# A new order table for a fused attention and gated MLP kernel: query-maxima splits on GpSimd, a weight load issued later

## The chip, the cores and the metric

The kernel runs on one core of a Trainium2 chip. The metric is the time of one execution on the device in microseconds (us); the number that counts is the median of several runs. Engine names are those of the profile: PE is TensorE (PEld its weight loads), DVE is VectorE, ACT is ScalarE, POOL is GpSimd, SP is SyncE, which here only issues transfers.

## The reference, cut to what matters

Two stages follow each other. The first is a linear attention over 8 batches, 8 heads, 576 tokens and head size 64, with a feature map of 2 x 128 features:

```python
def phi(x):
    proj = np.einsum('bhsd,df->bhsf', x, w_phi)
    proj = proj - np.max(np.abs(proj), axis=-1, keepdims=True)
    return np.concatenate([np.exp(proj), np.exp(-proj)], axis=-1)
q_p, k_p = (phi(q), phi(k))
kv = np.einsum('bhsf,bhsd->bhfd', k_p, v)
z = np.sum(k_p, axis=2)
num = np.einsum('bhsf,bhfd->bhsd', q_p, kv)
den = np.einsum('bhsf,bhf->bhs', q_p, z)[..., None] + 1e-06
```

Its output, heads side by side, is `x` of 8 x 576 x 512. The second stage is a gated MLP: `h = relu(x @ w_in)` with 1024 columns, split into `u` and `v` of 512; `v` is normalized over its columns, mixed over the tokens by the 576 x 576 matrix `w_spatial` plus a bias, multiplied with `u`, and multiplied by `w_out`.

## The kernel before

All work is written out as a list of words, `ORDER` (lines 17 to 153). The last lines of the kernel take the words one by one and call the function of that name, so the order of the words is the order of the instructions in each engine's queue; engines run their queues in order and wait for each other by semaphores that the framework sets. A word is a name, its indices, after a colon the buffers or PSUM banks that it takes, and after an @ the engine, where there is a choice: `qs.0.1.0:2@V` splits the maxima of batch 0, token half 1, head half 0 into buffer 2 on DVE. @V is DVE, @A ACT, @P POOL, @S SP. `BUFS` gives the number of buffers of each kind; a word that takes a buffer waits until the last reader of the earlier content is done.

The 576 tokens of a batch are four blocks of 128 and a tail of 64; the tails of two batches are worked on together (words that end in t, index g for the pair). The words of one batch, in the order of their data:

- Loads. `lk` and `lq` (lines 364 to 369) load keys and queries as bf16 from POOL's queue, `lv` values from SP's, `lkt`, `lqt`, `lvt` the tails. Batch 0 comes in pieces: `lkf` loads a quarter of the keys from SP, `ckf` casts it; `lq0` is half of the queries. `lin.0`, `lin.1` and `lout` load w_v, w_u and w_out, `lsp` the first 512 rows of the spatial weights, `lspt` (line 432) their last 64, all from POOL.
- Turns. `tk` and `tq` (line 491) transpose a piece on PE, `tkc` and `tqc` copy it out of PSUM. Later batches use transposes by transfer instead, `xk` and `xq` (line 481), from SP.
- Keys. `kp` (line 544) projects with w_phi into two banks, `km` (line 551) takes the absolute maxima on DVE, `ke` the two exponentials on ACT, `kem` (line 559) the exponentials of the maxima, with which `vs` (line 605) scales the values. `vsz` fills the columns for the sums, `vst` and `vstz` do the same for the tails. `kv` (line 628) multiplies features and values, `kvc` copies the result.
- Queries. `qp` projects, `qm` takes maxima, `qs` (line 650) splits the maxima into two bf16 parts: a cast and a subtraction, each of 128 x 8. `qt` turns the parts on PE, `qc` copies them, `qf` (line 660) projects again, transposed, and subtracts the maxima by matmuls, `qe` takes the exponentials. `qn` (line 712, matmuls at line 719) multiplies with kv, `qr` and `qx` divide.
- MLP. `tx`/`txc` on PE or `xx` by transfer transpose x; `vm` (line 832) computes v, `vr` its relu, `vb`, `va`, `vx`, `vw`, `vy`, `vn` normalize it; `um` and `ur` compute u; `sm` mixes over the tokens, `sg` gates, `om` multiplies by w_out, `oc` copies into one of five buffers `ob`, `od` stores it.
- `warm.n.w:b` is n filler matmuls of w columns on zeros into bank b. `zvst`, `zmhl`, `zsp`, `zvnt`, `csel`, `csel2`, `cphi`, `chalf` and `cident` make constants; `spt`/`spc` turn the spatial weights, `spb` adds their bias rows.

Around the start the queues stand like this. SP: the four quarters of the first keys, w_phi after the first, then the tails and values. POOL: the identity, `lspt`, the cast of the second key quarter (`ckf.1`), the queries of batch 0, `lsp`, `lk.1`, the last cast, `lin.0`, `lq.1`, `lin.1`, and only then products. DVE does the four splits of the main blocks of batch 0; POOL does the split of the tail and all splits of later batches.

The last output products (`om`) of the table come one after the other, each copied by ACT or DVE and stored by SP; the very last is `om.7.1`, copied by ACT.

Of the kernel before, what the change touches and what calls it, by code (L numbers as in the profile page):

```python
# [22 lines left out]
kpt.0:2,3 ket.0.0:0 cqt.0:0@V tqt.0:0 warm.2.512:1 tk.0.1.1:1 km.0.1:2 tqtc.0:0@V tkc.0.1.1@V csel2@V kem.0.2:1
kmt.0:3 ke.0.1.0:2 warm.3.512:0 warm.3.128:0 tq.0.0.0:0 ke.0.1.1 tqc.0.0.0:2@V tq.0.0.1:1 warm.11.128:1 qpt.0:6,7
kem.0.1:2 tqc.0.0.1@A warm.2.512:0 warm.1.128:0 qp.0.1.0:0,1 ke.0.2.1 zmhl.1@V tq.0.1.0:4 lvt.0:0@S lq.1:0 qmt.0:0
lv.0.1:1@S qp.0.0.0:6,7 tq.0.1.1:5 lbs:0@S lkt.1:0@S lin.1 qm.0.1.0:1 ket.0.1 tqc.0.1.0:3@A qm.0.0.0:2 kp.0.3:2,3
# [6 lines left out]
qc.0.1.1:2@V qet.0.1 qe.0.0.1.0:3 lv.1.0:3@S vs.0.3.1@P kv.0.3:4 kvc.0.3@A qe.0.0.1.1 qn.0.1.0:2,3 qr.0.0.0:0  # L33
lqt.1:1@S vsz.0.2@P qx.0.0.0:0 qf.0.1.1:6,7 vs.0.2.1@P qe.0.1.1.0:4 kv.0.2:4 qr.0.1.0:1 spt.4:0 tkc.1.0.0:4@V
qx.0.1.0:1 tk.1.0.1:1 lq.2:1 kvc.0.2@V spc.4@V lv.1.1:0@S qe.0.1.1.1 qnt.0.0:2,3 ckt.1:0@P qn.0.0.1:4,5 qrt.0.0:2
qxt.0.0:0 tk.1.1.0:0 vst.0.1.0@P lv.2.1:1@S qr.0.0.1:0 tkc.1.0.1@A qn.0.1.1:6,7 kp.1.0:2,3 qx.0.0.1 txt.0.0:1
qr.0.1.1:1 qx.0.1.1 tkc.1.1.0:5@V tx.0.0:4 tk.1.1.1:5 ke.1.0.0:4 txc.0.0:0@V warm.3.128:1 kp.1.1:6,7 tx.0.1:0
txtc.0.0:0@A km.1.0:1 tkc.1.1.1@V vst.0.1.1@V vm.0.0:1 xq.2.0:6 vmt.0.0:4 ke.1.1.0:0 txc.0.1@V spb@P tx.0.2:5 ke.1.1.1
warm.3.128:5 tx.0.3:0 km.1.1:2 vr.0.0:0@A kem.1.0:0 vm.0.1:1 tq.1.1.0:6 txc.0.3@V ke.1.0.1 txc.0.2@A vrt.0.0:1@A
tq.1.0.0:7 kem.1.1:2 tq.1.0.1:0 vm.0.2:2 vb.0.0:0 tq.1.1.1:3 va.0.0:0 lk.2:2 vr.0.1:2@A tqc.1.0.0:0@A vr.0.2:3@A  # L40
xq.2.1:1 tqc.1.0.1@A tqc.1.1.0:2@V tqc.1.1.1@A vm.0.3:1 vbt.0.0:1 vb.0.1:2 kp.1.3:4,5 vat.0.0:1 lout vs.1.0.0:1@P
qp.1.0.0:6,7 spt.3:0 vr.0.3:4@A va.0.1 vs.1.0.1@P vxt.0.0 vb.0.2:3 vs.1.1.0:0@P spc.3@A qp.1.0.1:2,3 vsz.1.1@P
vsz.1.0@P chalf@P vwt.0.0:0 ke.1.3.0:2 qm.1.0.0:1 vs.1.1.1@P lvt.1:0@S xk.2.0:3 xk.2.1:4 vx.0.0 va.0.2:2 um.0.0:1
kp.1.2:6,7 qm.1.0.1:2 vyt.0.0 kv.1.0:0 qs.1.0.0:1@P vb.0.3:0 ur.0.0:1@A ke.1.3.1 qt.1.0.0:1 lv.2.0:3@S spt.1:2 spt.0:3
qc.1.0.0:1@V spc.1@V um.0.3:1 vw.0.0:1 kvc.1.0:1@A ke.1.2.0:3 ke.1.2.1 tkt.1:0 va.0.3 ur.0.3@A vx.0.1 kv.1.1:2 vy.0.0
km.1.3:3 tktc.1:0@V vnt.0.0:0@P um.0.1:4 spt.2:5 spc.0@A spc.2@A vn.0.0:1@P kem.1.3:1 kvc.1.1@V qp.1.1.0:0,1 km.1.2:0
qm.1.1.0:3 vw.0.1:2 qf.1.0.0:2,3 qp.1.1.1:6,7 um.0.2:5 qs.1.0.1:0@P vy.0.1 kem.1.2:3 qt.1.0.1:0 qe.1.0.0.0:1 vn.0.3@P
vn.0.1@P vn.0.2@P sm.0.3:1 qm.1.1.1:0 qc.1.0.1:0@V qs.1.1.0:2@P ur.0.2@A sg.0.3 qt.1.1.0:5 sm.0.0:0 qf.1.0.1:6,7
qc.1.1.0:2@V vs.1.3.0:2@P lk.3:0 vsz.1.3@P qe.1.0.0.1 ur.0.1@A xk.3.1:5 qs.1.1.1:1@P qp.2.0.0:2,3 qe.1.0.1.0:0
vs.1.2.0:3@P qe.1.0.1.1 qp.2.1.0:4,5 vsz.1.2@P qm.2.0.0:1 qm.2.1.0:2 sg.0.0 sm.0.1:1 qt.1.1.1:2 vs.1.2.1@P sg.0.1  # L50
vs.1.3.1@P sm.0.2:3 qs.2.1.0:0@P qn.1.0.0:6,7 kv.1.2:4 qc.1.1.1:1@V lq.3:1 kv.1.3:5 kvc.1.3@A qp.2.0.1:0,1 qr.1.0.0:2
sg.0.2 kvc.1.2@A qf.1.1.0:2,3 qn.1.0.1:4,5 qx.1.0.0:2 qm.2.0.1:3 qe.1.1.0.0:3 qnt.0.1:6,7 qf.1.1.1:0,1 qe.1.1.0.1
# [10 lines left out]
qc.2.1.1:0@V qe.2.1.0.1 lv.4.1:0@S kp.2.3:4,5 vnt.0.1@P qe.2.0.0.0:0 km.2.3:1 qe.2.0.0.1 lq.5:0 vn.1.0:2@P vw.1.1:0
km.3.0:2 um.1.3:1 um.1.1:0 vsz.2.0@P od.0.1@S ur.1.3@A ur.1.1@A vy.1.1 vn.1.1@P vn.1.3@P vn.1.2@P qp.3.0.0:2,3
kem.2.3:1 ke.2.3.0:3 ke.3.0.0:2 smt.0.1:1 vs.2.0.1@P xk.4.1:6 vs.2.1.0:0@P sm.1.2:0 qm.3.0.0:2 sgt.0.1 qp.3.0.1:2,3
sg.1.2 smt.0.0:1 vs.2.1.1@P qm.3.0.1:1 ke.3.0.1 vsz.2.1@P ke.2.3.1 kem.3.0:2 vs.2.3.0:3@P sm.1.0:0 qf.2.0.1:6,7
qpt.1:2,3 vsz.2.3@P kem.2.2:3 vs.2.3.1@P vs.2.2.0:2@P xk.4.0:4 sg.1.0 sgt.0.0 kp.3.1:4,5 kv.2.0:0 lv.3.1:3@S
qe.2.0.1.0:2 od.0.2@S kvc.2.0:2@A vs.2.2.1@P qe.2.0.1.1 kv.2.1:1 kvc.2.1@A kv.2.3:0 qmt.1:3 km.3.1:0 kvc.2.3@A
qp.3.1.1:2,3 kp.3.3:6,7 vsz.2.2@P qm.3.1.1:0 ke.3.1.0:1 ke.3.1.1 sm.1.3:1 kv.2.2:0 lq.4:1 km.3.3:1 qn.2.0.0:2,3
kvc.2.2@A sg.1.3 qr.2.0.0:1 sm.1.1:4 ke.3.3.0:4 qs.3.0.0:2@P qx.2.0.0:1 kem.3.3:1 qt.3.0.0:5 qc.3.0.0:2@V kem.3.1:3  # L70
qn.2.0.1:0,1 qr.2.0.1:2 omt.0:5 vs.3.0.0:1@P qp.3.1.0:2,3 ke.3.3.1 oct.0:3@A kp.3.2:6,7 vs.3.0.1@P qx.2.0.1 od.0.0@S
sg.1.1 qm.3.1.0:2 ke.3.2.0:3 qst.1:1@P qf.2.1.1:0,1 vs.3.1.0:0@P om.1.1:4 vst.1.1.0@P om.1.2:5 qe.2.1.1.0:3 km.3.2:2
oc.1.1:0@A qe.2.1.1.1 xx.2.0:2 oc.1.2:4@V om.1.3:2 qtt.1:3 ke.3.2.1 qn.2.1.0:4,5 oc.1.3:2@V qct.1:1@V qf.3.0.0:0,1
qr.2.1.0:0 qn.2.1.1:2,3 qs.3.1.0:0@P ckt.2:0@V qx.2.1.0:2 vs.3.1.1@P qr.2.1.1:1 qx.2.1.1 om.1.0:6 qe.3.0.0.0:4
qft.1:4,5 qs.3.0.1:2@P kem.3.2:0 vs.3.3.0:3@P vsz.3.1@P kp.4.0:2,3 kv.3.1:7 oc.1.0:1@V vsz.3.0@P km.4.0:3 vsz.3.3@P
vs.3.3.1@P xq.5.1:0 qe.3.0.0.1 qet.1.0:0 kv.3.0:6 vm.2.1:0 qet.1.1 qt.3.0.1:1 kvc.3.0:0@V kvc.3.1@A odt.0@S ke.4.0.0:0
# [978 lines left out]
```

## Time and profile before

| | |
|---|---|
| median of 3 runs | 264.83 us (264.47 to 265.33) |
| the profiled execution | 264.12 us |
| its span, first to last instruction | 262.3 us |
| PE busy | 247.9 us, 94% of the span |
| DVE busy | 220.1 us, 84% |
| ACT busy | 200.7 us, 77% |
| POOL busy | 168.4 us, 64% |
| bytes moved | 41.91 MB, 160 GB/s in the mean |

Busy times are sums of instruction times. PE's are modelled at their ends and overlap, so PE may show busy while it only finishes; the fillers count as busy too. A row of the timeline has the start, the duration, the engine, the line, the operation, the output and inputs by the names of the program, the count, and in brackets the idle time of that engine before it and what ended it. The line is often that of a helper: 267 is every copy on DVE or POOL, 265 every copy on ACT, 547 every projection, 552 every maximum.

### The profile page before, as it was taken

Reading aid. Unit: us, or ns where it says so; the run is one execution under the profiler, and the core shown is the slowest. Engines: PE = TensorE matmul, PEld = TensorE weight load, DVE = VectorE, ACT = ScalarE, POOL = GpSimd, SP = SyncE. Lnnn points to the kernel's source line nnn. Section 1 sums busy time; section 2 is a strip of 40 time slices with the busy share of each in tenths; the row PEclk is TensorE's granted clock in tenths of the full one; section 3 lists DMA queues with packets and bytes.
Section 4 is the critical chain, followed back from the end, with each engine's and each line's share of the span. In section 5 each row is a group of like instructions: output and inputs, shape, how many; then the busy total and the mean of one; then the engine's idle time right before and its main releaser. Section 6 shows DMA issues by size and latency. Waiting matters only on the chain.

```text
span 262.3 us, 8256 instructions
## 1 busy us (share of the span) xinstructions
PE 247.9 (94%) x3292; PEld 151.6 (58%) x3329; DVE 220.1 (84%) x441; ACT 200.7 (77%) x332; POOL 168.4 (64%) x300
## 2 busy tenths in 40 slices
...
GB/s 162 212 203 224 225 219 262 152 161 214 122 173 199 181 236 142 130 145 175 157 219 314 153 146 171 60 182 193 189 177 81 90 75 2 40 82 0 122 189 214
DMA packets 82076, 41.91 MB, mean 160 GB/s; under 512 B 50995, under 2 KB 77299, under 8 KB 82037
## 3 DMA queue, kind: packets, MB, share of 16 engines
...
q8 instruction: 26, 0.43, 0.7%
...
## 4 chain that ended last, share of the span: by engine, by line
PE 61%; DVE 16%; DMA 14%; issue 3%; ACT 3%; SPq 1%; DVEq 0%; ACTq 0%
PE banks L834 8%; PE banks L959 8%; PE banks L945 8%; PE banks L930 8%; DMA tf<-in_q_dram 6%; PE banks L547 5%; PE banks L636 5%; DVE mk L552 4%; PE banks L719 4%; DMA T<-ld 4%; DMA out_dram<-ob 3%; DVE mq L552 3%; PE banks L663 3%; PE banks L667 2%; PE banks L947 2%
## 5 line engine op out<-in xcount | busy, mean ns | idle before, releaser
L672 ACT ACTIVATE qf<-banks 128x1024 bf16<-128x1024 f32 x72 | 70.2, 1030 | 7.5 <-PE banks L667 6.7
L556 ACT ACTIVATE kf<-banks 128x1024 bf16<-128x1024 f32 x64 | 64.1, 1034 | 7.8 <-PE banks L547 3.8
L605 POOL TENSOR_TENSOR vs<-v,em 128x512 bf16<-128x512 f32 x63 | 64.9, 1039 | 7.9 <-ACT em L562 6.3
L552 DVE TENSOR_REDUCE mq<-banks 128x8 f32<-128x1024 f32 x36 | 43.2, 1213 | 2.9 <-PE banks L547 2.6
L552 DVE TENSOR_REDUCE mk<-banks 128x8 f32<-128x1024 f32 x36 | 43.3, 1213 | 1.4 <-PE banks L547 0.8
L945 PE MATMUL banks<-w_spT,vn 128*128 128x512 bf16 x119 | 32.1, 380 | 0.5
L930 PE MATMUL banks<-xT,w_u 128*128 128x512 bf16 x128 | 32.2, 380 | 0.1
L843 POOL TENSOR_TENSOR rs<-mv,neghalf 128x2 f32<-128x2 f32 (+2 forms) x21 | 13.9, 666 | 28.5 <-DVE mv L840 28.3
L834 PE MATMUL banks<-w_v,xT 128*128 128x512 bf16 x117 | 30.9, 379 | 0.6
L959 PE MATMUL banks<-w_out,uT 128*128 128x512 bf16 x119 | 29.8, 379 | 0.5
L954 DVE TENSOR_TENSOR uT<-banks,uT 128x512 bf16<-128x512 f32 x32 | 21.3, 680 | 6.8 <-PE banks L947 6.7
L547 PE MATMUL banks<-wphi,T 64*128 64x128 bf16 x512 | 23.9, 218 | 2.6 <-ACT uT L271 1.5
L271 ACT ACTIVATE vr<-banks 128x512 bf16<-128x512 f32 (+1 forms) x27 | 16.3, 604 | 11.8 <-PE banks L834 7.8
L849 POOL TENSOR_SCALAR vn<-vr,rs,mv 128x512 bf16<-128x512 bf16 x30 | 23.0, 774 | 1.3 <-POOL mv L846 0.2
L636 PE MATMUL banks<-vs,kf 128*128 128x66 bf16 x512 | 23.3, 194 | 0.1
L636 PEld LDWEIGHTS <-kf 128*128 128x128 bf16 x512 | 21.4, 97 | 2.6
L861 DVE BATCH_NORM_STATS2 st<-vr 128x6 f32<-128x512 bf16 x32 | 21.5, 682 | 1.4 <-ACT vr L271 1.1
L547 PEld LDWEIGHTS <-T 64*128 64x128 bf16 x512 | 15.5, 94 | 12.2 <-issue 9.5
L732 DVE TENSOR_TENSOR x<-banks,rc 128x512 bf16<-128x512 f32 x32 | 21.9, 686 | 0.7
L265 ACT COPY ob<-banks 128x512 f32<-128x512 f32 x19 | 11.0, 591 | 14.7 <-PE banks L959 14.2
L638 PE MATMUL banks<-vst,kft 128*128 128x66 bf16 x128 | 20.9, 192 | 0.0
L719 PE MATMUL banks<-kv,qf 128*128 128x66 bf16 x512 | 20.7, 193 | 0.0
...
## 6 DMA issues: line engine op xcount, KB each, us to landing
v<-in_v_dram SPq DMA_DIRECT2D x16, 512.0 KB, 9.1
...
ld<-in_k_dram POOLq DMA_DIRECT2D x7, 512.0 KB, 9.3
ld<-in_q_dram POOLq DMA_DIRECT2D x7, 512.0 KB, 9.2
...
```

What stands on the lines that cost most here:

```text
L547: nc.tensor.matmul(out=bank(banks[y])[:, n * F:(n + 1) * F], lhsT=xT[halves[y], n, :], rhs=wphi[halves[y], :], start=True, stop=True)
L552: nc.vector.tensor_reduce(out=out_, in_=pp.rearrange("p y (n f) -> p y n f", f=F), axis=AX.X, op=ALU.max, apply_absolute_value=True)
L556: nc.scalar.activation(out=kf[:, s].rearrange("p y n f -> p y (n f)"), in_=pp, func=AF.Exp, bias=0.0, scale=(1.0, -1.0)[s])
L605: ENG[e].tensor_tensor(out=at["vs", (b, j)][:, s, :, 0:D], in0=at["v", (b, j // 2)][:, (j % 2) * n:(j % 2 + 1) * n, :], in1=at["em", (b, j ...
L636: nc.tensor.matmul(out=pv[:, hh, s, :], lhsT=kf[:, s, c % 2, 2 * hh + c // 2, :], rhs=w[:, s, NB * hh + c, :], start=(c == 0), stop=False)
L672: nc.scalar.activation(out=at["qf", u][:, s].rearrange("p y n t -> p y (n t)"), in_=at["pq", u], func=AF.Exp, bias=0.0, scale=(1.0, -1.0)[s])
L719: nc.tensor.matmul(out=at["pn", u][:, y, n, :], lhsT=f[:, s, y, n, :], rhs=at["kv", b][:, hg * HH + n, s, :], start=(s == 0), stop=(s == 1))
L834: nc.tensor.matmul(out=bank(place)[r], lhsT=lhs[:, kc, r], rhs=w_v[:, kc, :], start=(kc == 0), stop=(kc == KC - 1))
L849: ENG[e].tensor_scalar(out=out_, in0=in_, scalar1=rs, scalar2=mv, op0=ALU.mult, op1=ALU.add)
L930: nc.tensor.matmul(out=bank(place).rearrange("p (c t) -> p c t", c=NB), lhsT=w_u[:, kc, dc * P:(dc + 1) * P], rhs=at["xT", b][:, :, kc, :] ...
L945: nc.tensor.matmul(out=bank(place), lhsT=at["vn", b][:, c, cs], rhs=w_spT[:, c, 0:T0], start=(c == 0), stop=False)
L959: nc.tensor.matmul(out=bank(place), lhsT=at["uT", b][:, dc, c * P:(c + 1) * P], rhs=w_out[:, dc, :], start=(dc == 0), stop=(dc == KC - 1))
```

## The change

Only the table is another. It holds the same words but for the fillers, in another order, with some other buffers and banks, and with other engines for some words. By the fillers it has 1,504 words instead of 1,498: 41 filler matmuls of 512 columns instead of 39, and 36 of 128 columns instead of 48.

Engines: the four splits `qs.0.1.0`, `qs.0.0.0`, `qs.0.1.1` and `qs.0.0.1` go from DVE to POOL, so that all 36 splits are there. Three products `vs.0.1.1`, `vs.0.3.0` and `vs.0.3.1` go from POOL to DVE, `vs.0.2.0` from DVE to POOL. `ckf.2` (ACT), `ckf.3` (POOL) and `ckt.0` (ACT) go to DVE, `ckt.1` from POOL to ACT, `zvnt.1` from DVE to ACT. Of the copies of kv DVE does 21 instead of 13, of the outputs `oc` 13 instead of 16; some others of the copies and relus change in both directions.

Order: on POOL, `lspt` moves behind `ckf.1`, the two `lq0`, `chalf` and `lk.1`; `lin.1` moves from behind `lq.1` to behind `vsz.0.3`. SP's queue is the same up to `lv.0.1`. On DVE, `zmhl.0` and `csel` stand ahead of the first cast, `zvst` and `csel2` behind the first turn copy. Words that consume a transfer stand on average further behind it: `oc.2.0`, `oc.2.1` and `oc.2.3`, for instance, stood 49, 185 and 44 words behind the store that frees their buffer, and now stand 54, 137 and 55 words behind it.

The first lines of the table, then those of the stores in the middle, and its end:

```diff
-lkf.0:0,0@S lphi@S lkf.1:1@S lkf.2:2@S zblank@V cident ckf.0@V warm.7.512:0 warm.2.128:0 tk.0.0.0:0 cphi@V lspt:3
-zvst.0@V ckf.1@P tkc.0.0.0:0@V lq0.0.4:1 zsp@V csel zvnt.0@A ckf.2@A warm.4.512:1 warm.2.128:1 kp.0.0:2,3 km.0.0:0
-zmhl.2@V lq0.4.4 warm.3.512:0 warm.2.128:0 tk.0.1.0:0 ke.0.0.0:0 tkc.0.1.0:1@V zvnt.1@V lkt.0:0@S tk.0.0.1:1 zmhl.0@V
...
-qs.0.1.0:0@V vs.0.1.0:0@P qs.0.0.0:1@V qst.0:2@P qtt.0:4 vs.0.0.0:1@P warm.4.512:0 warm.1.128:0 qt.0.1.0:0 tqc.0.1.1@A
-ke.0.3.0:3 vs.0.1.1@P kemt.0:3 qc.0.1.0:0@V qp.0.1.1:6,7 vs.0.0.1@P ke.0.3.1 qm.0.1.1:3 vsz.0.1@P vst.0.0.0:0@P
-qt.0.0.0:5 vsz.0.0@P vstz.0@P qf.0.1.0:0,1 qe.0.1.0.0:0 vst.0.0.1@P qct.0:1@V warm.13.128:5 qp.0.0.1:6,7 km.0.3:0
-qm.0.0.1:0 qc.0.0.0:2@A qe.0.1.0.1 warm.2.512:4 warm.1.128:4 qf.0.0.0:4,5 qft.0:2,3 qs.0.1.1:2@V kem.0.3:2
-qe.0.0.0.0:1 qs.0.0.1:0@V warm.3.512:0 warm.2.128:0 kv.0.0:0 qt.0.0.1:1 qe.0.0.0.1 vs.0.3.0:2@P vsz.0.3@P kvc.0.0:0@V
-lv.3.0:2@S qc.0.0.1:0@V kv.0.1:6 kvc.0.1@V vs.0.2.0:3@V qt.0.1.1:4 qf.0.0.1:0,1 tk.1.0.0:5 qn.0.0.0:6,7 qet.0.0:2
...
+zblank@V cident zmhl.0@V csel lkf.0:0,0@S lphi@S lkf.1:1@S ckf.0@V ckf.1@P lq0.0.4:1 lq0.4.4 chalf@P warm.7.512:0
+warm.2.128:0 tk.0.0.0:0 zvnt.1@A tkc.0.0.0:0@V warm.5.512:1 warm.1.128:1 tk.0.0.1:0 zvst.0@V csel2@V cphi@V zsp@V
+warm.2.512:1 warm.2.128:1 kp.0.0:2,3 zmhl.1@V lkf.2:2@S ckf.2@V warm.2.512:1 warm.2.128:1 tk.0.1.0:1 tkc.0.0.1@V
+zvnt.0@A kp.0.1:4,5 zmhl.2@V ke.0.0.0:0 lkt.0:0@S tkc.0.1.0:1@V warm.1.512:0 warm.2.128:0 kp.0.2:6,7 km.0.1:0
+lqt.0:1@S ke.0.0.1 lk.1:2 ckt.0:0@V ke.0.2.0:1 km.0.0:1 lspt:3 kem.0.1:0 warm.5.512:0 warm.3.128:0 tkt.0:0 ke.0.2.1
+tktc.0:0@V ke.0.1.0:2 lsp:0 cqt.0:0@V lin.0 warm.5.512:1 warm.1.128:1 kpt.0:2,3 tqt.0:0 warm.4.512:1 warm.3.128:1
...
+qst.0:0@P ke.0.3.0:3 warm.1.512:0 warm.1.128:0 qtt.0:0 kem.0.2:3 ke.0.3.1 qct.0:0@A ket.0.1 tq.0.1.0:1 qs.0.1.0:1@P
+qm.0.0.0:2 vs.0.0.1@P tqc.0.1.0:3@V qt.0.1.0:0 vsz.0.0@P km.0.3:0 qft.0:4,5 qs.0.0.0:2@P qc.0.1.0:1@A tq.0.1.1:1
+qet.0.0:0 tqc.0.1.1@V warm.4.512:2 warm.1.128:2 qp.0.0.1:2,3 qt.0.0.0:0 vs.0.1.1@V lv.0.1:1@S kem.0.3:1 qm.0.0.1:3
+qf.0.1.0:6,7 vst.0.0.0:0@P vstz.0@P qet.0.1 lkt.1:0@S vst.0.0.1@P qp.0.1.1:4,5 qc.0.0.0:2@A qm.0.1.1:0 vsz.0.1@P
+qf.0.0.0:0,1 qs.0.1.1:0@P vst.0.1.1@V qs.0.0.1:1@P warm.2.512:2 warm.1.128:2 kv.0.0:2 qe.0.1.0.0:1 kv.0.1:3 qt.0.1.1:4
+lbs:0@S kvc.0.0:0@V tk.1.0.0:5 qt.0.0.1:2 vs.0.2.0:2@P qe.0.0.0.0:2 qe.0.0.0.1 kvc.0.1@V qe.0.1.0.1 tkc.1.0.0:4@V
+vsz.0.2@P qn.0.0.0:0,1 vs.0.2.1@P qc.0.0.1:0@V vs.0.3.0:3@V qf.0.0.1:2,3 qr.0.0.0:0 qc.0.1.1:1@A qx.0.0.0:0 vsz.0.3@P
+qf.0.1.1:6,7 vs.0.3.1@V qe.0.0.1.0:3 qe.0.1.1.0:4 qe.0.1.1.1 lin.1 qn.0.1.0:4,5 qe.0.0.1.1 vst.0.1.0@P qr.0.1.0:1
...
-vr.3.2:3@A kem.4.2:1 qm.4.0.1:3 vr.3.3:1@A sm.2.3:0 um.3.0:1 od.1.0@S vb.3.0:1 kmt.2:2 qt.4.0.0:4 vb.3.2:0 vb.3.3:2
-kemt.2:0 ket.2.1 va.3.2:3 sm.2.0:5 od.1.2@S lq.6:1 sg.2.3 va.3.0:4 ur.3.0:1@A va.3.3 vx.3.1 qc.4.0.0:0@V va.3.1
...
+warm.4.128:3 qn.3.0.0:6,7 qe.3.0.1.1 qrt.1.2:2 qxt.1.2:0 od.1.0@S qn.3.0.1:0,1 tkt.2:2 vm.2.2:3 qe.3.1.0.0:2 va.2.0:0
...
+vnt.1.2:1@P sm.2.2:7 kmt.2:3 vb.3.1:0 lqt.2:1@S sg.2.2 kem.4.0:2 sm.2.1:6 sg.2.1 od.1.2@S ket.2.0:0 lvt.2:0@S lk.6:0
+va.3.1 vx.3.0 qs.4.0.1:0@P vs.4.0.0:1@P vw.3.0:4 od.0.0@S sm.2.3:0 sm.2.0:1 qm.4.1.1:1 qt.4.0.1:7 vm.3.2:6 sg.2.3
...
-odt.3@S om.7.2:0 oc.7.3:3@A oc.6.3:1@V om.7.0:1 od.6.2@S oc.7.2:4@A od.6.3@S oc.7.0:2@A od.7.3@S od.7.2@S od.7.0@S
-om.7.1:0 oc.7.1:0@A od.7.1@S
...
+sg.7.1 sg.7.3 om.7.3:2 om.7.2:3 om.7.0:4 oc.6.3:1@A oc.6.2:3@A oc.7.3:0@V om.5.2:2 od.6.3@S oc.7.2:4@A od.6.2@S
+od.7.3@S oc.7.0:2@V od.7.2@S oc.5.2:1@A od.7.0@S om.7.1:0 od.5.2@S oc.7.1:3@A od.7.1@S
```

More of the change, by code (lines that the diff above doesn't have):

```diff
@@ L23 @@
[L23 to L26, printed above, removed]
-qs.0.1.0:0@V vs.0.1.0:0@P qs.0.0.0:1@V qst.0:2@P qtt.0:4 vs.0.0.0:1@P warm.4.512:0 warm.1.128:0 qt.0.1.0:0 tqc.0.1.1@A
@@ L33 @@
[L33 to L52, printed above, removed]
@@ L63 @@
[L63 to L76, printed above, removed]
-qc.3.0.1:0@V vr.2.1:1@V qt.3.1.0:4 qs.3.1.1:1@P qc.3.1.0:2@V vs.3.2.0:2@P vm.2.0:5 qf.3.0.1:6,7 ke.4.0.1 vs.3.2.1@P
```

199 lines of the change are left out of this document (116 added, 83 removed).

## The prediction, as it was put on record

> **What bounds the kernel now.** I read the page first, then busy time by stretch, then the timeline of the first 46 us, the waits, and the chain.
>
> ```profile
> PE 247.9 (94%) x3292; PEld 151.6 (58%) x3329; DVE 220.1 (84%) x441; ACT 200.7 (77%) x332; POOL 168.4 (64%) x300
> 0.00:40.00 40.00, 35.18 (x484) 22.92 (x489) 33.15 (x66) 29.98 (x49) 25.41 (x42) 1.00 1.11 207
> 40.00:118.00 78.00, 76.44 (x1136) 48.67 (x1145) 73.94 (x146) 70.50 (x119) 58.02 (x107) 1.00 1.25 176
> 118.00:142.00 24.00, 21.73 (x201) 11.20 (x202) 20.43 (x38) 16.61 (x31) 19.25 (x35) 1.00 1.19 211
> 142.00:228.00 86.00, 84.54 (x1286) 53.72 (x1301) 75.61 (x152) 73.10 (x118) 55.32 (x99) 1.00 0.62 126
> L348 PE MATMUL banks<-blank 128*128 128x512 bf16 x36 | 12.1, 455 | 1.7 <-DVE blank L343 1.2 <-DVE tT L267 0.4 <-issue 0.2
> ```
>
> In a stretch row the columns are its length, then PE, PEld, DVE, ACT and POOL busy, the granted clock, the share of the transfer engines (above 1 where packets overlap) and GB/s. The row to see is the first: of 40 us PE shows 35.2 busy, but a third of that is filler (L348, the `warm` words, whose group alone is 12.1 us and which nearly all stand before 42 us). From 40 us on PE is 98% busy but for 118 to 142, where 2.3 us are missing, and DVE is at 95% beside it. So the 218 us behind 40 are real PE work in a fixed amount. What a new order of the same operations can move is the start, the few PE stalls in the middle, and the tail.
>
> What ends the waits in the start:
>
> ```profile
> PE banks L658 <- DVE mhl L654: 2.4, 3, 1.2
> L653 DVE CAST mhl<-mq 128x8 bf16<-128x8 f32 x4 | 2.3, 587 | 0.0
> L654 DVE TENSOR_TENSOR mhl<-mq,mhl 128x8 bf16<-128x8 f32 x4 | 2.2, 562 | 0.1
> L653 POOL CAST mhl<-mq 128x8 bf16<-128x8 f32 x32 | 6.0, 188 | 14.9 <-DVE mq L552 14.8
> L654 POOL TENSOR_TENSOR mhl<-mq,mhl 128x8 bf16<-128x8 f32 x32 | 6.4, 201 | 2.6
> 20.84 1.03 POOL L618 TENSOR_TENSOR vst<-vt,em 64x512 bf16<-64x512 f32 x1
> 20.95 0.95 DVE L654 TENSOR_TENSOR mhl<-mq,mhl 128x8 bf16<-128x8 f32 x1
> ```
>
> In the first row the numbers are total, times and longest. The four splits that DVE does (2.3 + 2.2 = 4.5 us for eight tiny operations) end the largest sum of PE waits that one cause has in this trace (2.4); on POOL the same pair takes 0.39. The last two rows say why: a DVE split of 8 columns lasts until POOL's product, begun before it, is over (20.95 + 0.95 against 20.84 + 1.03).
>
> **The change, part by part.** The functions stay; only the word order, some engines and some buffers differ. The words are the same operations, so I count what each queue loses and gains ahead of three places.
>
> ```profile
> 1.18 3.38 PE L348 MATMUL banks<-blank 128*128 128x512 bf16 x9 [1.18 <-DVE blank L343]
> 3.42 0.43 DVE L267 CAST ld<-ob 128x512 bf16<-128x512 f32 x1 [2.30 <-DMA ob<-in_k_dram]
> 4.35 0.63 PE L495 MATMUL banks<-ident,ld 128*128 128x128 bf16 x4
> 4.89 0.23 DVE L267 CAST wphi<-wphi_f 128x128 bf16<-128x128 f32 x1 [1.03 <-DMA wphi_f<-in_w_phi_dram]
> 5.28 0.94 DVE L330 MEMSET vst<- 128x1056 uint32 x1 [0.17 <-issue]
> 5.94 0.60 POOL L267 CAST ld<-ob 128x512 bf16<-128x512 f32 x1 [3.75 <-DMA ob<-in_k_dram]
> 6.14 0.36 DVE L267 COPY T<-banks 128x512 bf16<-128x512 bf16 x1
> 6.63 0.40 PE L547 MATMUL banks<-wphi,T 64*128 64x128 bf16 x8
> 27.45 0.43 DVE L267 CAST kv<-banks 128x264 bf16<-128x264 f32 x1
> 29.21 0.67 PE L719 MATMUL banks<-kv,qf 128*128 128x66 bf16 x16
> 37.65 1.04 PE L834 MATMUL banks<-w_v,xT 128*128 128x512 bf16 x3
> L317 DVE TENSOR_SCALAR sel<-sel 128x512 bf16<-128x512 bf16 x1 | 0.4, 408 | 0.0
> L267 DVE COPY vnt<-ident 128x512 bf16<-128x512 bf16 x2 | 1.1, 596 | 0.0
> ```
>
> First projection (kp.0.0, now 6.63). PE does the same nine fillers and the first turn to 4.98. The copy of it no longer stands behind the 0.94 memset (5.03 instead of 6.14), but that memset, csel2 (0.41) and cphi (0.23) now stand before wphi is ready, at 6.9; PE meanwhile has five fillers, the second turn and four more fillers, and gets to kp.0.0 at about 7.5: 0.9 late. The load of the spatial tail rows leaves the first 6 us; at best the second key block comes earlier for it (its cast waited 3.75 for the load and ended at 6.54). But PE does not reach the turn that reads that block before 6.8, so these fillers hide it, and I take nothing.
>
> DVE up to the first kv copy (kvc.0.0, now 27.45). Both queues hold the same ten reductions. Gone are the four splits (4.5), the two vnt copies of zvnt.1 (1.2) and two mT copies, qc.0.1.0 and qct.0 (0.5 by ACT's row below). Turn copies: two go (tkc.0.1.1, tqc.0.0.0), two come (tqc.0.1.0, tqc.0.1.1). New are three casts of 128x512 (ckf.2, ckf.3, ckt.0; 1.3 at 0.43) and two products, vs.0.1.1 and vst.0.1.1.
>
> ```profile
> L605 DVE TENSOR_TENSOR vs<-v,em 128x512 bf16<-128x512 f32 x1 | 0.7, 681 | 0.0
> L605 POOL TENSOR_TENSOR vs<-v,em 128x512 bf16<-128x512 f32 x63 | 64.9, 1039 | 7.9 <-ACT em L562 6.3 <-issue 1.3
> 15.97 3.49 DVE L552 TENSOR_REDUCE mq<-banks 128x8 f32<-128x1024 f32 x3 [0.33 <-PE banks L547]
> 25.08 3.77 ACT L672 ACTIVATE qf<-banks 128x1024 bf16<-128x1024 f32 x4
> 10.83 0.31 ACT L562 ACTIVATE em<-mk 128x8 f32<-128x8 f32 x2
> 15.57 0.58 ACT L265 COPY T<-banks 128x512 bf16<-128x512 bf16 x1
> 23.70 0.26 ACT L265 COPY mT<-banks 128x128 bf16<-128x128 bf16 x1
> ```
>
> With 0.68 for each product the new work is 2.7, against 6.2 gone: 3.5 us net leave this queue. A walk through the five queues with these durations (reductions 1.17 in series, from 3.49 for three) leaves DVE waiting about 0.5 before qm.0.1.0 (for ACT's copy tqc.0.0.1), 0.4 before qm.0.1.1, and 1.1 at the first turn, and puts kvc.0.0 at about 26: 1.5 early.
>
> ACT over the same stretch becomes the next bound. From ke.0.0.0 (8.0) to the exponential that the first sums need (qe.0.0.0.1) it has 15 exponentials at 1.0 (four took 3.77), five pairs of em (0.31), three turn copies (0.58) and three mT copies (0.26): 15 + 1.6 + 1.7 + 0.8 = 19.1, so 27.1. The first sums (L719, qn.0.0.0) start at about 27.0 instead of 29.2. They stand one features block (0.45) earlier in PE's order, so the lead is 1.75. The next block, from kp.1.0 over tx.0.0, gives the first w_v product (L834, vm.0.0) at about 36.1 instead of 37.65, with one turn of x (0.2) more already done: a lead of 1.7, and 1.7 is what I take for the start. Ends: 2.2, where the ACT sum alone decides, and a loss, below.
>
> POOL pays four splits (1.56) and gets rid of two vs (2.08), ckf.3 and ckt.1. Its order now waits at vs.0.0.0 for kem.0.0 (17.3) and at qs.0.1.1 for DVE; behind that stand vs.0.2.0 and vs.0.2.1, done at 29.0, when kv.0.2 is wanted at 29.1. Nothing is hidden beyond that 0.1.
>
> The load of w_u (lin.1) moves behind vsz.0.3, from 14.6 to about 30:
>
> ```profile
> w_u<-in_moe_w_in_dram POOLq DMA_DIRECT2D x1, 512.0 KB, 22.7
> w_out<-in_moe_w_out_dram POOLq DMA_DIRECT2D x1, 512.0 KB, 14.7
> 14.60 0.76 POOL L421 DMA_DIRECT2D w_u<-in_moe_w_in_dram  x1
> ```
>
> Its 22.7 us came behind six other large loads of that queue; at 30 fewer stand ahead, as for w_out (14.7). Then it lands at 44.7 by w_out's row, 52.7 by its own; um.0.0 comes at about 44. By the nearer row 0 to 0.7; I take nothing and keep the rest as a rival.
>
> The middle. The longest PE stall behind 40 us lies in 118 to 142:
>
> ```profile
> 130.26 8.49 DMA out_dram<-ob
> 138.85 0.69 DVE L267 COPY ob<-banks 128x512 f32<-128x512 f32 x1 [2.24 <-DMA out_dram<-ob]
> 139.33 0.38 PE L547 MATMUL banks<-wphi,T 64*128 64x128 bf16 x7 [1.54 <-ACT uT L271]
> ```
>
> It is a buffer: oc.2.0 takes the one that od.1.0 reads, 49 words later in the table, and the transfer needed 8.5 us. In the new table od.1.0 stands 137 words before its successor, and the two near pairs (od.0.0, od.1.2) 54 and 55, on ACT instead of DVE. At about 5.7 words per us (1,498 in 262) that is 9.5 us, just over 8.5. I take 0.7 of the 1.54 back (ends 0 and 1.54). Elsewhere in 40 to 228 I take nothing: DVE has 1.6 us more to do there (eight more copies of kv at 0.43, three fewer of outputs, and the like), under 1% of the 170 that the three stretch rows show.
>
> Two groups of late fillers are new, six of 128 columns:
>
> ```profile
> 22.67 0.90 PE L348 MATMUL banks<-blank 128*128 128x128 bf16 x13
> ```
>
> At 0.07 each (13 took 0.90) they cost 0.4. In the tail PE now has no stall that the waits show; both tables end in an output product, an ACT copy and od.7.1. The new one has tight hand-overs (om.6.0 behind ur.7.3 and sg.6.3, smt.3.1 behind vn.7.1, all on DVE) and seven output products in the last run instead of six: 0.2 (0 to 0.8).
>
> Sum, against the profiled execution's 264.12 (span 262.3): 264.12 - 1.7 - 0.7 + 0.4 + 0.2 = 262.3. The median of the three runs is 0.71 above that execution; a median may lie so again, so I add half: 262.6.
>
> **Rivals.** (1) The products on DVE wait for POOL: slower. Three vs and vst.0.1.1 now run on DVE while POOL is in a chain of products; the old trace has no product on DVE beside one on POOL. If they wait as the splits did, each waits for the rest of a product of 1.04 us, 4.2 at the most, in front of qm.0.0.1 and of kv.0.3: 262.3 + 4.2 = 266.5. It turns the sign from 1.8 of waiting on. For it: the rows 20.84 and 20.95. Against it: only one POOL operation is in the way each time, about half of it on average, and two of the four come when POOL waits for em or a maximum.
>
> [...]
>
> (2) The lead is given back, no change: loads and transposes of 40 to 140 come when buffers fall free, and land as late as before (8.5 for an output); an earlier PE only waits for them. 1.7 + 0.7 go: 264.7. For it: the share of the transfer engines is above 1 up to 142 us. Against: PE was 98% busy there with those same transfers.
>
> (3) w_u lands by its own row: um.0.0 waits 8.7 us, 271. Against: w_out's row, and that the 22.7 hold the turns of the loads that were issued just before it.
>
> **Numbers.** Forecast 0.54 (own range 260.2 to 264.0), no change 0.20, DVE products 0.14, w_u or another new wait of the middle 0.09, better than 260.2 0.03. Range 260.2 (2.2 + 1.54 gained, no price) to 266.6. A run of this kernel can tell 0.3%, 0.8 us, from no change. Faster 0.56, same 0.20, slower 0.24.
>
> **What would show it.** Right: no DVE row at L653 and L654, 36 on POOL; first L719 near 27, first L834 near 36, with kp.0.0 later than 6.63; no PE wait of over 1 us at 130 to 140. Wrong: DVE rows at L605 and L618 well over 0.69, or L930 waiting for w_u, or PE idle from 40 to 228 us above the 5.3 that the three stretch rows show now.

## The result, and the profile after

| | before | after |
|---|---|---|
| median (4 runs each) | 264.94 us (264.47 to 265.33) | 261.45 us (260.05 to 262.03) |
| ratio after to before | | 0.9861 (95% interval 0.9814 to 0.9909) |
| the profiled execution | 264.12, span 262.3 | 260.05, span 258.3 |

Faster, by 3.5 us in the medians. The forecast was 262.6 and 2.2 faster; the time lies in its range, which with 260.2 to 266.6 is wide enough to hold no change as well. Ratios in this document leave out single runs more than 1.5% above the fastest of their kernel, and they are estimates of their own, not quotients of the medians, which count all runs. The profiled execution of the new kernel happens to be the fastest of its four, so its gain of 4.07 overstates the median's.

First the new kernel's page and its stretches, with the columns of the stretch rows shown before:

```profile
PE 244.8 (95%) x3282; PEld 150.8 (58%) x3319; DVE 220.6 (85%) x440; ACT 200.0 (77%) x329; POOL 168.7 (65%) x304
```
```profile
40.00:118.00 78.00, 76.23 (x1144) 49.05 (x1155) 75.09 (x149) 70.66 (x115) 58.17 (x106) 1.00 1.15 175
118.00:142.00 24.00, 23.79 (x222) 12.25 (x223) 23.05 (x43) 19.54 (x38) 19.26 (x37) 1.00 1.14 228
142.00:228.00 86.00, 84.90 (x1292) 54.86 (x1307) 74.71 (x158) 70.50 (x113) 59.45 (x108) 1.00 0.65 134
```

PE's missing 2.27 us of 118 to 142 have become 0.21; the other two stretches hardly changed (76.44 and 84.54 before). Now the splits, the product groups and PE's wait for the splits, from the groups by line and shape:

```profile
L653 POOL CAST mhl<-mq 128x8 bf16<-128x8 f32 x36 | 7.3, 204 | 6.3 <-DVE mq L552 3.8 <-PE banks L658 1.9 <-DVE mT L267 0.3
L658 PE MATMUL banks<-ident,mhl 128*128 128x128 bf16 x36 | 7.8, 221 | 0.5 <-POOL mhl L654 0.3
L605 DVE TENSOR_TENSOR vs<-v,em 128x512 bf16<-128x512 f32 x3 | 2.8, 922 | 0.0
```

No DVE split is left, and PE's 2.4 us of waiting for splits are 0.3. The DVE products take 0.92 in the mean instead of 0.68. The marks of the start, from the timeline:

```profile
7.75 0.40 PE L547 MATMUL banks<-wphi,T 64*128 64x128 bf16 x8
18.99 0.43 PE L348 MATMUL banks<-blank 128*128 128x512 bf16 x2 [1.13 <-DVE mq L552]
25.88 0.77 DVE L267 CAST kv<-banks 128x264 bf16<-128x264 f32 x2
26.72 0.67 PE L719 MATMUL banks<-kv,qf 128*128 128x66 bf16 x16
36.75 1.04 PE L834 MATMUL banks<-w_v,xT 128*128 128x512 bf16 x3
```

They answer to 6.63, 27.45, 29.21 and 37.65 of before. The second row is PE's longest wait between 7 and 28 us: fillers that wait until DVE has read their bank.

The end, from the two chains of waits (start and duration of the last run of output products), the old kernel first:

```profile
252.93 5.21 PE banks L959 x24
```
```profile
247.07 6.06 PE banks L959 x28
```

The last product ends at 258.14 before and at 253.13 after, 5.0 earlier; the span ends only 4.0 earlier. About 1 us was given back behind the last product in this pair.

### The profile page after: what moved, and what is told of

It reads as the page before. It is cut to its first block, busy times and chain, and to the rows that moved or that the text cites. A ratio compares the mean times of both kernels' runs of the same rounds, so it can differ in the third digit from the quotient of the medians.

```text
span 258.3 us, 8229 instructions
## 1 busy us (share of the span) xinstructions
PE 244.8 (95%) x3282; PEld 150.8 (58%) x3319; DVE 220.6 (85%) x440; ACT 200.0 (77%) x329; POOL 168.7 (65%) x304
## 4 chain that ended last, share of the span: by engine, by line
PE 75%; DVE 10%; DMA 4%; issue 3%; POOL 3%; ACT 2%; SPq 1%; DVEq 0%; ACTq 0%; POOLq 0%
PE banks L834 11%; PE banks L930 10%; PE banks L959 9%; PE banks L945 9%; PE banks L547 6%; PE banks L636 5%; PE banks L719 5%; DVE mq L552 3%; DMA ld<-in_q_dram 3%; PE banks L663 3%; PE banks L667 3%; PE banks L947 2%; DVE mk L552 2%; PE banks L991 2%; POOL vs L605 2%
## 5 line engine op out<-in xcount | busy, mean ns | idle before, releaser
L605 POOL TENSOR_TENSOR vs<-v,em 128x512 bf16<-128x512 f32 x61 | 62.7, 1041 | 5.1 <-ACT em L562 2.4
L265 ACT COPY ob<-banks 128x512 f32<-128x512 f32 x21 | 12.4, 597 | 17.1 <-PE banks L959 11.9
L547 PE MATMUL banks<-wphi,T 64*128 64x128 bf16 x512 | 23.3, 218 | 0.1
L719 PEld LDWEIGHTS <-qf 128*128 128x128 bf16 x512 | 19.1, 98 | 3.8 <-issue 0.2
```

The lines of the kernel that those rows point to most:

```text
L547: nc.tensor.matmul(out=bank(banks[y])[:, n * F:(n + 1) * F], lhsT=xT[halves[y], n, :], rhs=wphi[halves[y], :], start=True, stop=True)
L605: ENG[e].tensor_tensor(out=at["vs", (b, j)][:, s, :, 0:D], in0=at["v", (b, j // 2)][:, (j % 2) * n:(j % 2 + 1) * n, :], in1=at["em", (b, j ...
L719: nc.tensor.matmul(out=at["pn", u][:, y, n, :], lhsT=f[:, s, y, n, :], rhs=at["kv", b][:, hg * HH + n, s, :], start=(s == 0), stop=(s == 1))
```

## The experiments

Each kernel was timed next to the kernel before on its own chip. The rows of the table stand in that order: the first four share one chip (before: 264.15 us, 30 runs), the next four another (264.49, 33 runs), the last four a third (264.32, 20 runs). Only ratios are compared across chips. "Low clock" counts the runs whose mean granted TensorE clock was 0.994 or less. In the first eight kernels the table takes more lines, so that a line number in their rows is 2 higher than in the kernel before (1 higher with the sixth buffer).

| kernel | median us (runs) | ratio to before (95%) | low clock |
|---|---|---|---|
| new start, old rest (`start_new`) | 261.80 (8) | 0.9942 (0.9915 to 0.9969) | 0 of 8 |
| old start, new rest (`rest_new`) | 263.43 (12) | 0.9985 (0.9960 to 1.0011) | 6 of 12 |
| new, splits on DVE (`after_qs_dve`) | 262.95 (12) | 0.9979 (0.9953 to 1.0006) | 7 of 12 |
| old, splits on POOL (`before_qs_pool`) | 264.99 (11) | 1.0039 (1.0009 to 1.0070) | 8 of 11 |
| new table again (`after_2`) | 262.07 (10) | 0.9892 (0.9852 to 0.9932) | 2 of 10 |
| old, more fillers (`before_fill`) | 263.81 (12) | 0.9974 (0.9950 to 0.9998) | 1 of 12 |
| old, cast later (`before_cqt`) | 263.86 (12) | 0.9988 (0.9960 to 1.0017) | 2 of 12 |
| old, sixth buffer (`before_ob6`) | 263.91 (12) | 0.9979 (0.9952 to 1.0007) | 4 of 12 |
| new, products on POOL (`after_vs_pool`) | 260.27 (6) | 0.9869 (0.9827 to 0.9910) | 0 of 6 |
| new, old tail (`tail_old`) | 260.91 (6) | 0.9875 (0.9837 to 0.9912) | 0 of 6 |
| old, the three edits (`before_repaired`) | 263.33 (12) | 0.9965 (0.9941 to 0.9988) | 0 of 12 |
| new start, two edits (`start_repaired`) | 262.03 (9) | 0.9915 (0.9878 to 0.9952) | 0 of 9 |

The kernel before shows a low clock in 43 of its 83 runs on the three chips (16 of 30, 18 of 33, 9 of 20).

**Which half of the table.** `start_new` is the new table up to word 350 and the old order behind it; `rest_new` is the reverse.

```diff
 (start_new) new table to qc.1.1.1, then the old order of the words still missing
-lv.3.0:2@S qe.1.1.1.0:4 xq.3.0:2 xk.4.1:6 xq.4.0:1 xq.4.1:2
+lv.3.0:3@S qe.1.1.1.0:3 xq.3.0:6 xk.4.1:1 xq.4.0:2 xq.4.1:6
```

> The new table up to qc.1.1.1 (its first 350 words without the fillers), then the old order for all the rest; six words get another buffer and lv.4.1 stands 35 words later, since the buffers of the two parts would collide. In the two profiled executions the new table leads by 1.6 us of the same PE work at 70 us and by 4.7 behind 150 us. My theory: the start gives its 1.6 us and they last to the end, while the two waits of the middle (0.58 at 123.7 and 1.54 at 139.3) stay, because the old distances between stores and copies stay: 1.2 to 2.0 us faster than before, and the wait of about 1.5 at the store still in the profile near 138. Rival one, the lead is given back behind transfers that land as late as before: within 0.5 us of before. Rival two, the waits of the middle vanish already because the start has moved against the transfers: 3 us or more faster.

> The old table up to qc.1.1.1 (its first 351 words without the fillers), then the new order for all the rest; 15 words get another buffer or bank and xq.3.1 stands ten words later. My theory: the new rest saves the PE waits of 118 to 160 us (about 2.9 us by the stretch rows) and gives 0.7 back in the last stores: 1.7 to 2.5 us faster than before. Rival, the start is the cause of both: under 0.7 us faster. First w_v product (L834) still at about 37.6 us, as before.

The new start alone is 0.6% faster (0.3 to 0.9), 1.5 us: the first theory's size. Part of that expectation failed: its profile shows no wait near 138. The wait of 0.58 at 123.71 is still there, and one is new, both on transfers:

```profile
122.02 0.40 PE L549 MATMUL banks<-wphi,T 64*128 64x128 bf16 x8 [0.56 <-DMA T<-ld]
125.95 1.90 PE L836 MATMUL banks<-w_v,xT 128*128 128x512 bf16 x8 [0.51 <-DMA xT<-x]
```

The new rest behind the old start gains nothing that can be told from zero (0.4 us by the ratio, 0.7 in the medians), which is the rival's size; there the theory fell. The stretches in the one profile of `rest_new` (length, PE busy, clock, share of the transfer engines, GB/s) show where the gain goes:

```profile
40.00:118.00 78.00, 75.38 (x1109) 1.00 1.07 165
118.00:142.00 24.00, 23.74 (x240) 1.00 1.24 215
```

It does save the 2 us of 118 to 142, but PE is 1.06 less busy from 40 to 118 than in the old order. And the clock falls in its start, to 0.50 from 22 to 24 us, as in the next experiments.

**The splits.** `after_qs_dve` and `before_qs_pool` change nothing but the four engines:

```diff
 (after_qs_dve; before_qs_pool is the reverse, in the old table)
-qs.0.1.0:1@P  qs.0.0.0:2@P  qs.0.1.1:0@P  qs.0.0.1:1@P
+qs.0.1.0:1@V  qs.0.0.0:2@V  qs.0.1.1:0@V  qs.0.0.1:1@V
```

> The new table with the four splits back on DVE, nothing else. My theory: the splits on DVE stand behind POOL's products again and cost the start about what the change gained there: 1.0 to 2.5 us slower than the new table (about 262.5 to 264 us), with DVE rows at L653 and L654 of 0.4 us and more in the mean. Rival, ACT's 19 us of exponentials bound the start and hide the splits: within 0.5 us of the new table.

> The old table with the four splits on POOL, nothing else. If the splits alone make the start's gain: 1.2 to 2.0 us faster than before, first L719 near 27.5 instead of 29.2. Rival, in the old order POOL is inside a run of products of 1.04 us each when a maximum is ready, so that a split waits there for up to three of them and the gain is eaten: within 0.5 us of before.

Without the move of the splits nearly all of the gain is gone: 0.9979 of before instead of 0.9861 and 0.9892 (other chips), 2.3 to 3.1 us. In its profile one subtraction takes 1.18 and PE gets to the first sums at 30.37 instead of 26.72. Not all of these 3.65 us are the splits: 0.71 was there at 15.50 already, where PE waited for a load of queries, and the clock is at 0.50 from 22 to 24 us and at 0.70 from 24 to 26.

```profile
22.79 1.18 DVE L656 TENSOR_TENSOR mhl<-mq,mhl 128x8 bf16<-128x8 f32 x1
30.37 0.83 PE L721 MATMUL banks<-kv,qf 128*128 128x66 bf16 x16
```

But the move alone is a loss, 0.4% (0.1 to 0.7). Neither theory had it so. In the old order the split of `qs.0.1.0` stands first in POOL's queue, and its maximum is the third that DVE computes; POOL waits 3.25 us with all its products behind it, then PE 2.26:

```profile
19.46 0.19 POOL L655 CAST mhl<-mq 128x8 bf16<-128x8 f32 x1 [3.25 <-DVE mq L554]
21.84 0.23 PE L660 MATMUL banks<-ident,mhl 128*128 128x128 bf16 x1 [2.26 <-POOL mhl L656]
```

So the engine change doesn't pay in the old order, and the new order hardly pays without it.

**The clock.** The same kernel shows what came behind its gap. Stretches of `before_qs_pool` (PE alone: length, busy, granted clock, share, GB/s):

```profile
20.00:22.00 2.00, 0.17 (x2) 1.00 1.25 248
22.00:24.00 2.00, 2.00 (x16) 0.66 1.26 226
24.00:26.00 2.00, 2.00 (x21) 0.50 1.22 196
26.00:28.00 2.00, 1.95 (x33) 0.99 1.31 191
```

PE waits 2.26 us up to 21.84, and then its clock falls: the three windows behind that lack 1.70 us of full clock in sum. Taken as two levels, 1.00 and 0.50 (at the end of the new kernel's trace windows of 0.25 us read 1.00 up to 256.25, one 0.90, then 0.50), it was at 0.50 for 3.4 us, an estimate: all of the window with 0.50, 1.36 us of the one with 0.66 and 0.04 of the last. The old start has a gap of nearly that size (1.15 and 0.59 us in its two waits for DVE splits). Windows in the profile of `rest_new`, whose start is the old one, and in that of the kernel before:

```profile
18.00:20.00 2.00, 1.23 (x10) 1.00 1.28 200
20.00:22.00 2.00, 0.93 (x12) 0.99 1.25 251
22.00:24.00 2.00, 1.79 (x21) 0.50 1.24 220
24.00:26.00 2.00, 1.94 (x19) 0.65 1.23 195
```
```profile
18.00:20.00 2.00, 1.64 (x18) 1.00 1.25 179
20.00:22.00 2.00, 0.60 (x10) 1.00 1.27 243
22.00:24.00 2.00, 2.00 (x33) 1.00 1.23 240
24.00:26.00 2.00, 1.95 (x25) 1.00 1.22 197
```

The same words with the same gap (1.84 and 1.76 us idle from 18 to 22): in one execution the clock fell, in the other not. The prediction was made from the second. `before_fill` puts fillers into the gap:

```diff
-vs.0.0.0:1@P warm.4.512:0 warm.1.128:0 qt.0.1.0:0
+vs.0.0.0:1@P warm.9.512:0 warm.1.128:0 qt.0.1.0:0
...
-vst.0.0.0:0@P qt.0.0.0:5
+vst.0.0.0:0@P warm.3.512:5 qt.0.0.0:5
```

> The old table with eight more fillers of 512 columns: warm.4.512:0 ahead of qt.0.1.0 becomes warm.9.512:0, and warm.3.512:5 stands ahead of qt.0.0.0, where PE otherwise waits 1.15 and 0.59 us for the splits on DVE. About half of the 30 runs of the old kernel show a mean granted clock of 0.994 or less, median 264.4 us against 263.1 us of the others; three profiles with such a clock show it at 0.72 to 0.85 from 20 to 28 us, right behind that gap. Theory: the gap makes the clock fall, and the new table gains a part of its time by having no gap there. Then no run shows a clock below 0.995 and the median is 0.4 to 1.0 us faster than before. Rival, the clock falls for another reason (or for the work itself): as many low clocks as before, and the median the same or 0.3 us slower.

One low clock in 12 instead of 18 in 33, and 0.26% faster (0.02 to 0.50), 0.7 us. That one run is the profiled one. Its clock is 1.00 from 18 to 28 us and falls behind the other stall of the old order, where PE is idle for 2.0 of 3 us:

```profile
138.00:141.00 3.00, 1.00 (x19) 1.00 0.97 342
141.00:144.00 3.00, 2.78 (x28) 0.54 0.79 206
```

So a low mean clock doesn't say where the clock fell, and the old order has two places for it. `before_cqt` and `before_ob6`, tested below, keep the gap at 20 us and change only what PE waits for near 139; they have 2 and 4 low clocks in 12. The counts therefore don't show which gap is behind most of the 18. That a fall can follow the gap at 20 us is shown by the profile of `rest_new`.

The runs of before with a low clock have medians 1.0 to 1.3 us above the others on all three chips (264.46 against 263.17, 265.15 against 264.13, 264.56 against 263.57). In `after_qs_dve` the two kinds don't differ (262.95 and 262.94). In the profile of `rest_new` 1.84 us of idle time in 4 stood ahead of the fall; why it came there and not behind the 1.76 of the kernel before is not shown.

**The stall near 139 us.** PE's wait there names ACT's relu, and the forecast blamed the store that held DVE's copy at that moment. ACT's rows in the kernel before:

```profile
138.16 0.62 ACT L265 CAST tl<-tf 128x512 bf16<-128x512 f32 x1 [1.83 <-DMA tf<-in_q_dram]
138.69 0.59 ACT L271 ACTIVATE uT<-banks 128x512 bf16<-128x512 f32 x1
```

The relu stands behind the cast of the tail queries, which waits for another transfer.

```diff
 (before_cqt)
-cqt.2:0@A om.2.1:5 ur.3.1@A oc.2.1:3@V
+om.2.1:5 ur.3.1@A cqt.2:0@A oc.2.1:3@V
 (before_ob6, with BUFS ob=6)
-oc.2.0:1@V
+oc.2.0:5@V
```

> The old table with cqt.2 on ACT behind ur.3.1 instead of in front of it. In the old profile PE waits 1.54 us at 139.33 for ACT's relu ur.3.1, which stands behind the cast of the tail queries, and that cast waits 1.83 for its transfer; at the same time DVE waits 2.24 for a store to free the buffer of oc.2.0. Theory: the cast is the cause of PE's wait; then PE's wait near 138 goes and the time falls by 0.7 to 1.5 us. Rival (the forecast's reading): the store is the cause; then PE still waits 1 us or more there and the time stays within 0.4 us.

> The old table with a sixth buffer ob, taken by oc.2.0, which then waits for no store. By the forecast's reading the PE wait of 1.54 us at 139.33 goes or halves and the time falls by 0.7 to 1.5 us. By the rival, that the cast of the tail queries on ACT is the cause, PE's wait stays at 1 us or more and the time within 0.4 us of before.

With the cast moved, PE waits 0.47 instead of 1.54, now for DVE's copy, that is for the store:

```profile
139.15 1.02 PE L932 MATMUL banks<-xT,w_u 128*128 128x512 bf16 x4 [0.47 <-DVE ob L269]
```

So in this pair of profiles the cast was two thirds of the stall and the store the rest behind it (the tail queries also landed a little earlier here: their cast starts at 137.79 instead of 138.16). `before_ob6` doesn't tell them apart: in its profile the tail queries came in time (the cast waited 0.40), and no wait is left. Neither edit moves the time measurably; with all three small edits:

> The old table with the three small edits together: the eight fillers in the gaps of the splits, cqt.2 behind ur.3.1, and a sixth buffer for oc.2.0. If the gain of the new table comes from the gap at 20 us (through the clock) and from the stall at 138 us alone: as fast as the new table, 2.3 us or more faster than before. If its shorter start is a part of its own (1.4 us in the runs without a low clock): 1.0 to 1.8 us faster than before, and no mean clock below 0.995.

> The new start up to qc.1.1.1 with the old rest, and in that rest cqt.2 behind ur.3.1 and a sixth buffer for oc.2.0. Theory, the start and the stall near 138 us add up: 2.0 to 3.3 us faster than before, as the new table or better. Rival, the time saved at 138 is lost to transfers that land at their own time: as the new start alone, 1.3 to 1.9 us faster by the ratio.

`before_repaired` is 0.35% faster (0.12 to 0.59), 0.9 us, with no low clock: a little under the second case. The new start is a part of its own, as `start_repaired` shows: 0.85% (0.5 to 1.2), 2.2 us, and a median of 262.03 against 263.33 of `before_repaired` on the same chip, with no low clock in either. Whether the two edits add to the new start's 0.6% can't be told (the intervals meet).

**What is left of the middle.** `after_2` is the new table itself.

> The new table once more, only broken into other lines, as the measure for the edits on the same chip. The new start with the old rest took 261.8 us where the old kernel took 264.15. If the two halves of the table add up (2.35 and 0.7 us in the medians), 3.0 us faster than before here; if the new rest only pays after a new start, 3.5 us or more; if the first result was chance, 2.3 us or less.

It is 2.9 us faster than before by the ratio (1.8 to 3.9), so the expected cases can't be told apart. By the ratios the two halves alone add up to 0.7%, and the whole table gains 1.1 to 1.4% in its two measurements; the intervals meet, so that the new rest pays more behind the new start is likely, but not shown. Its profiled execution took 262.32 us, with a wait that the first profile doesn't have:

```profile
129.44 1.90 PE L836 MATMUL banks<-w_v,xT 128*128 128x512 bf16 x8 [1.57 <-DMA xT<-x]
```

That transposing transfer kept SP 4.12 us and began at 121.10, right behind another of 5.06; in the first profile the two took 2.77 and 2.59:

```profile
115.95 5.06 SPq L483 DMA_TRANSPOSE T<-ld  x1
121.10 4.12 SPq L797 DMA_TRANSPOSE xT<-x  x1
```
```profile
115.02 2.59 SPq L481 DMA_TRANSPOSE T<-ld  x1
120.26 2.77 SPq L795 DMA_TRANSPOSE xT<-x  x1
```

The ten runs spread accordingly: four from 259.69 to 260.21, the other six from 261.98 to 263.59. The two profiles are one of each kind, and two kernels below with the same middle add one of each: in `after_vs_pool` (262.63) a transposing transfer of 8.81 us, from 114.35, stands in the chain that ended last and this w_v product begins at 130.17, in `tail_old` (260.31) no transfer is among the longest pieces of the chain there and it begins at 127.23 (127.04 in the first profile). So the late product goes with 2.0 to 2.6 us in four profiles of four. What makes the transfers slow stays open, and that this wait alone makes the difference is argued.

**Products and tail.**

```diff
 (after_vs_pool, in the new table)
-vs.0.1.1@V  vs.0.3.0:3@V  vs.0.3.1@V  vst.0.1.1@V  vs.0.2.0:2@P
+vs.0.1.1@P  vs.0.3.0:3@P  vs.0.3.1@P  vst.0.1.1@P  vs.0.2.0:2@V
 (tail_old: new table for 1190 words, then the old order)
```

> The new table with five products on the engines of the old one: vs.0.1.1, vs.0.3.0, vs.0.3.1 and vst.0.1.1 on POOL, vs.0.2.0 on DVE. In the new profile the DVE products next to POOL products take 1.08, 0.83 and 0.85 us instead of 0.68, so they do wait for POOL, but only 0.7 in sum. Theory: this hurts little, and POOL, busy with hardly a pause from 16.9 to 29.8, would deliver vs.0.3.1 some 3 us later with three more products: 0.5 to 2 us slower than the new table, 0.5 to 2.5 faster than before. The forecast's rival (1), that the products on DVE cost up to 4 us of waiting for POOL: faster than the new table by 0.5 us or more.

> The new table for its first 1190 words (fillers not counted, to about 205 us), then the old order to the end; four words get another buffer or bank. In the profiles the time from the last weight load to the end of the span is 5.7 us in the new one, 4.8 in the old. Theory: the new tail costs 0.5 to 0.9 us (seven products in its last run instead of six, the last copies close together), against the 0.2 of the forecast: that much faster than the new table, 3 to 4 us faster than before. Rival, the difference is chance: 2.3 to 2.9 us faster than before, as the new table itself.

One of the five goes further than the old engines: vst.0.1.1 was on DVE in the old table too, only behind kvc.0.0. With the products on POOL the start is later, as the theory said: PE waits 1.20 ahead of the first sums and begins w_v at 37.91 instead of 36.75.

```profile
28.09 0.23 PE L658 MATMUL banks<-ident,mhl 128*128 128x128 bf16 x1 [1.20 <-DVE kv L267]
37.91 1.04 PE L834 MATMUL banks<-w_v,xT 128*128 128x512 bf16 x4
```

Yet it is not slower (0.9869; its interval meets both of the new table's). About half of the 1.16 is not the products: 0.56 is there at 15.35, where PE waited for a load of queries. In `after_2`, with the products on DVE, PE got past that load at 15.65, and its first w_v products in the chain start 0.84 later than in the first profile (39.00 instead of 38.16), so w_v began at about 37.6, an estimate. That leaves 0.6 for the edit; where it is made good stays open, and the new table itself ran on other chips. `tail_old` is as fast as the new table too. Neither beats it beyond the intervals.

## Why the prediction was right, step by step

The sum gave 1.8 us against the profiled execution, 2.2 against the median; 3.5 was measured at first and 2.9 in `after_2`. The sign and the main term, the start, are right. What the sum lacks is the clock, and the cause that it gave for the stall in the middle is the smaller one of two.

- **The start (1.7 taken).** Right in its marks: kp.0.0 at 7.75 (7.5 forecast; 8.16 to 8.23 in five other profiles with these first words), kvc.0.0 at 25.88 (26), first sums at 26.72 (27.0). The first w_v product came at 36.75, not 36.1: a lead of 0.9 at that row. The new order has done more other work by then: counted in weight loads, each at the time of its kind, the lead at equal work is about 1.6 at 60 and 70 us, and 1.6 to 1.9 from 60 to 120 us in `start_new`, which goes on in the old order. In time the new start is worth 1.5 us by the ratio (0.8 to 2.2). In the runs without a low clock its medians lead by 1.4 (261.80 against 263.17) and, on the third chip, by 1.3 (262.03 against 263.33). So the mechanism holds, at a little less than its 1.7. The clock comes on top, and the prediction didn't have it, because its one profile shows 1.00 throughout: filling the gap at 20 us gained 0.7 us (0.1 to 1.3), of which 0.3 remains between the runs without a low clock (263.79 against 264.13). How the two add up can't be told: the medians of `start_new` lead by 2.35 in all, its ratio gives 1.5.
- **The second key block (nothing taken, hidden by fillers).** Wrong in the mechanism: PE does wait for it. The cast on POOL took 1.39 instead of 0.60 beside two DVE operations, one of which, the cast of w_phi, took 0.63 instead of 0.23. In the six profiles of this start PE waits 0.42 to 1.24 for it, in this one the longest.

```profile
5.43 1.39 POOL L267 CAST ld<-ob 128x512 bf16<-128x512 f32 x1 [4.13 <-DMA ob<-in_k_dram]
6.27 0.63 DVE L267 CAST wphi<-wphi_f 128x128 bf16<-128x128 f32 x1
6.88 0.40 PE L495 MATMUL banks<-ident,ld 128*128 128x128 bf16 x4 [1.24 <-POOL ld L267]
```

- **The w_u load (nothing taken).** Right. It landed 8.5 us after its issue at 29.77, at 38.3; rival (3) is out.

```profile
w_u<-in_moe_w_in_dram POOLq DMA_DIRECT2D x1, 512.0 KB, 8.5
```
```profile
44.34 1.02 PE L930 MATMUL banks<-xT,w_u 128*128 128x512 bf16 x4
```

- **The stall at 139 (0.7 taken of 1.54).** The wrong transfer: the cast on ACT held PE longer than the store did. The size was too small for the profile (2.06 of PE's idle time gone from 118 to 142). What it is worth in time is not shown: `before_cqt` and `before_ob6` gain 0.3 and 0.6 us by their ratios, neither beyond its interval, and in two of four profiles with the new middle a w_v product begins late, at 129 to 130. So the 0.7 is neither shown nor refuted.
- **The late fillers (0.4).** Too small to measure; the six are there.
- **The tail (0.2).** A little small, inside its 0 to 0.8. From the end of the last product to the end of the span (span less the last row of the chain) it is 4.3 us in the mean of eight profiles with the old tail (4.1 to 4.6) and 4.7 in five with the new (4.4 to 5.2): 0.4. In time it can't be told: `tail_old` is not faster than the new table.
- **Rival (1), the products.** The waits are real and small: the three vs took 1.08, 0.83 and 0.85 us, 0.7 in sum beyond 0.68 each, and vst.0.1.1, which was on DVE before as well and now stands earlier, none. It shows the other way too: two POOL copies of 0.21 took 0.68 and 0.67 beside DVE products (of 0.83 at 27.32 and 0.85 at 28.91). Whole-product waits, 4.2 in sum, did not come.

```profile
21.78 1.08 DVE L605 TENSOR_TENSOR vs<-v,em 128x512 bf16<-128x512 f32 x1
27.54 0.68 POOL L267 CAST vs<-em 128x32 bf16<-128x32 f32 x1
```

- **Rival (2), the lead given back.** Not for the whole table. The profile of `rest_new` shows it for the rest alone: what it saves at 118 to 142 it partly pays from 40 to 118.
- **A reading.** DVE at 95% beside PE holds for 40 to 118 us only; from 142 to 228 its row is 75.61 of 86, 88%. No term of the sum hangs on it.
